# The whole issue order of a routed-attention and feed-forward kernel replaced: same operations, engines and buffers, another order of all five queues

## The chip, the cores and the metric

The kernel runs on one core of a Trainium2 chip. The core has five instruction queues that run beside each other: TensorE (PE in the profile, its weight loads as PEld), VectorE (DVE), ScalarE (ACT), GpSimd (POOL) and SyncE (SP), which here only issues transfers. Each queue runs its instructions strictly in the order in which they were written, and waits on semaphores for what other queues or transfers deliver. The metric is the device time of one execution in microseconds (us); lower is better.

## The reference, cut to what matters

Two stages follow each other. The first is attention for 4 batches, 8 heads, 768 tokens and a head size of 64, in which a query sees only the keys of its own cluster (the nearest of 16 centroids). Its output, 3072 tokens of 512 values, goes through a feed-forward stage with a softmax gate and a layer norm.

```python
mask = q_assign[:, :, :, None] == k_assign[:, :, None, :]
scores = scale * np.matmul(q, k.transpose(0, 1, 3, 2))
scores = np.where(mask, scores, -1000000000.0)
attn = softmax(scores)                    # over the keys
x = np.matmul(attn, v)                    # 3072 x 512 after a reshape
h = x @ w_in                              # 3072 x 1024
solu = h * softmax(h)
ln = (solu - mu) / np.sqrt(var + 1e-06) * g_ln
out = ln @ w_out                          # 3072 x 512
```

## The kernel before

The heads are worked off in pairs, four pairs in each of the four batches. Each step of the kernel is a small function with a name, added to a table with its engine and what it needs. The names that matter here, with batch `b`, pair `p`, `i` = 0 for queries and 1 for keys:

- `ld b.p.i` loads tokens (L381 for batch 0; L412 for the later batches, in four parts for two pairs at once, the last part without a number: `ld1.0.0` is the last part of the queries of batch 1, `ld1.0.1` that of the keys). `lv` loads values (L558), `lo0` to `lo3` load w_out (L599), `li0` and `li1` load the two halves of w_in with a cast and are issued by POOL (L583).
- `tp` and `xa`/`xt` turn tokens in batch 0 (on PE, L395), `xt` turns them in later batches (on DVE, L420). `cl` multiplies by the centroids (PE, L469); `tb`, `mx`, `oh`, `ot` make the cluster masks (DVE); `pl` puts these rows below the tokens (L541); `ca` casts the tokens (L438, L440); `cv` casts values (L566).
- `S` multiplies scores (PE, L644), `E` is the exponential of 1024 columns (ACT, L654, 144 of them), `V` multiplies by the values into the one bank `ob` (PE, L666), `N` divides by the sums and so frees `ob` (DVE, L678 and L689).
- `me`, `mk`, `mf`, `km`, `ce` centre w_out once: `mk` (DVE, L614) copies a sum out, `mf` (PE, L617) multiplies that copy.
- Of the feed-forward stage, for 24 blocks of 128 tokens: `tx` turns x by a transfer, `h` is the first product (PE, L777), `hm` the maximum (DVE, L787), `ex` the exponential (ACT, L803), `u` a product (POOL, L810), `tu` a turn by a transfer, `y` the second product (PE, L849), `as`, `bn`, `ag`, `al` the norm, `sc` the scaling and `ou` the store.
- `z1` to `z5` and `sg` are small constants set by POOL (L1327, L1311).

What sets the order is one hand-kept list, `ORDER` (L38), of all 1562 names. `Weave.run` goes through it and calls each function, so that the list gives each of the five queues its order at once:

```python
for name in ORDER:
    o = self.ops[name]
    assert done.issuperset(o["first"]) and name not in done, name
    ...
    o["fn"]()
    done.add(name)
```

A second table, `AWAY`, gives some steps to another engine than usual. The scores have two buffers of 1024 columns in PSUM, so PE can be two regions ahead of ACT; the products `h` have one bank each for their two halves; token tiles have four buffers. Transfers issued by SP are written into hardware queues in SP's order; POOL's transfers have a queue of their own (q0 in the profile, against q1 for SP's).

Of the kernel before, what the change touches and what calls it, by code (L numbers as in the profile page):

```python
# [43 lines left out]
tp0.2.0.1 xa0.2.0 ot0.0.1 cl0.1 z1 pl0.0.1.0 pl0.0.0.1 pl0.0.0.0 cv0.0.0 pl0.0.1.1.0 xt0.2.0 S0.0
pl0.0.1.0.1 S0.1 pl0.0.1.1.1 tb0.1 tp0.2.1.0 pl0.0.1.0.0 E0 S1.0 xa0.2.1 tp0.2.1.1 ca0.1.0.1 S1.1
xt0.2.1 cv0.0.1 tp0.3.0.0 ca0.2.0.0 S2.0 E1 mx0.1 S2.1 cl0.2 z4 oh0.1 ca0.2.1.0 E2 xa0.3.0 S3.0
S3.1 ot0.1 V0.0 tp0.3.0.1 E3 ca0.1.1.0 S4.0 S4.1 xt0.3.0 V0.1 ca0.2.1.1 V1.0 E4 V1.1 tb0.2 S5.0 lo0
S5.1 z2 pl0.1.1.1 N0 tp0.3.1.0 E5 S6.0 pl0.1.1.0 xa0.3.1 S6.1 V2.0 lo3 V2.1 mx0.2 pl0.1.0.1 E6
tp0.3.1.1 ld1.0.0.2 pl0.1.0.0 S7.0 ca0.1.1.1 gt xt0.3.1 S7.1 lv0.2 cv0.1.1 V3.0 V3.1 gk oh0.2 S8.0
E7 ca0.3.0.0 S8.1 cl0.3 N1 E8 ot0.2 cv0.1.0 S9.0 S9.1 gw V4.0 V4.1 E9 S10.0 pl0.2.0.1 pl0.2.0.0  # L50
S10.1 tb0.3 V5.0 ld1.0.0 V5.1 E10 sg S11.0 pl0.2.1.0 ld1.0.1.0 ca0.2.0.1 S11.1 N2 me0 E11 mx0.3
pl0.2.1.1 V6.0 V6.1 oh0.3 ca0.3.0.1 S12.0 S12.1 ca0.3.1.0 V7.0 S13.0 E12 ld1.0.1.1 S13.1 ot0.3
ca0.3.1.1 cv0.2.0 me1 E13 pl0.3.0.0 S14.0 pl0.3.1.0 cv0.2.1 lv0.3 S14.1 mk V7.1 E14 pl0.3.1.1 S15.0
N3 S15.1 mf z3 ld1.0.1.2 pl0.3.0.1 E15 ld1.0.1 S16.0 km S16.1 V8.0 V8.1 E16 li0 S17.0 ce2 S17.1
V9.0 V9.1 E17 S18.0 N4 S18.1 li1 ld1.2.0.0 E18 S19.0 S19.1 cv0.3.0 cv0.3.1 xt1.0.0 ld1.2.0.1 E19
V10.0 V10.1 ce1 V11.0 V11.1 S20.0 N5 S20.1 S21.0 E20 S21.1 V12.0 V12.1 xt1.0.1 E21 V13.0 S22.0
S22.1 ce3 ca1.0.1.0 V13.1 E22 S23.0 N6 S23.1 cl1.0 xt1.1.0 E23 ce0 S24.0 S24.1 ptx0 xt1.1.1 V14.0
V14.1 E24 V15.0 S25.0 S25.1 tx0 V15.1 E25 z5 ca1.1.0.0 S26.0 N7 S26.1 cl1.1 ce5 E26 tb1.1 S27.0
S27.1 tb1.0 V16.0 V16.1 E27 S28.0 mx1.0 S28.1 V17.0 V17.1 ld1.2.0.2 E28 ca1.0.0.0 S29.0 N8 S29.1
h0.0.0 oh1.0 E29 V18.0 ld1.2.0 S30.0 S30.1 h0.0.1 ot1.0 E30 S31.0 S31.1 ld1.2.1.0 V18.1 ce4 V19.0  # L60
E31 pl1.0.0.0 V19.1 S32.0 S32.1 N9 h0.1.0 ld1.2.1.1 E32 hm0.0 S33.0 pl1.0.1.1 S33.1 V20.0 h0.1.1
E33 ld1.2.1.2 pl1.0.1.0 S34.0 S34.1 V20.1 V21.0 E34 V21.1 pl1.0.0.1 S35.0 ld1.2.1 N10 S35.1 h1.0.0
E35 ca1.0.1.1 hm0.1 S36.0 S36.1 lv1.0 V22.0 xt1.2.0 h1.0.1 bl1.0 E36 S37.0 S37.1 hm1.0 ca1.0.0.1
V22.1 tx2 V23.0 E37 V23.1 S38.0 N11 S38.1 ca1.1.1.0 h1.1.0 E38 lv1.1 S39.0 ca1.2.0.0 S39.1 h1.1.1
tx4 E39 xt1.2.1 S40.0 ca1.1.1.1 S40.1 E40 hm1.1 cl1.2 xt1.3.0 cv1.0.0 ex0.0 S41.0 S41.1 cv1.0.1
V24.0 V24.1 tb1.2 V25.0 V25.1 E41 V26.0 u0.0 S42.0 V26.1 S42.1 N12 h2.0.0 E42 h2.0.1 xt1.3.1 V27.0
h2.1.0 ex1.0 ce6 tu0 S43.0 hm2.0 S43.1 h2.1.1 E43 V27.1 S44.0 hm2.1 ld2.0.0.0 S44.1 h3.0.0 E44
ld2.0.0.1 bn0.0 cl1.3 u1.0 bn0.1 lv1.2 ex2.0 V28.0 V28.1 tb1.3 S45.0 V29.0 V29.1 mx1.2 ld2.0.0.2
S45.1 h3.0.1 ca1.2.1.0 E45 ld2.0.0 S46.0 S46.1 oh1.2 h3.1.0 ca1.3.0.1 E46 y0.0 N13 h3.1.1 cv1.1.1
S47.0 S47.1 bn1.0 ca1.1.0.1 cv1.1.0 ld2.0.1.0 y0.1 E47 hm3.0 S48.0 S48.1 y0.2 ot1.2 E48 tu1 V30.0  # L70
S49.0 S49.1 ce7 V30.1 V31.0 E49 V31.1 ld2.0.1.1 S50.0 as0 as1 ca1.2.0.1 pl1.2.0.1 bn1.1 S50.1
h4.0.0 ld2.0.1.2 E50 hm3.1 S51.0 pl1.2.1.1 S51.1 V32.0 ag0 V32.1 E51 y0.3 pl1.2.1.0 N14 S52.0 S52.1
h4.0.1 ld2.0.1 pl1.2.0.0 al0 E52 S53.0 as2 S53.1 bl1.2 V33.0 u2.0 V33.1 E53 h4.1.0 lv1.3 hm4.0
# [1285 lines left out]
```

## Time and profile before

| | before |
|---|---|
| time, median of 3 runs | 220.64 us (220.5 to 221.01) |
| profiled execution, span from first to last instruction | 224.4 us |
| PE busy | 213.4 us (95%) |
| ACT busy | 190.0 us (85%) |
| DVE busy | 182.4 us (81%) |
| POOL busy | 162.3 us (72%) |
| moved by transfers | 37.28 MB, 120878 packets |

The profile gives the span alone for the profiled execution; it is 3.8 us longer than the median of the timed runs, although the span holds nothing ahead of the first or behind the last instruction. Busy time of PE is modelled at its ends: a matmul that waits inside the pipe counts as busy. Idle time of an engine is put down to what released it last.

### The profile page before, as it was taken

The page shows a single profiled execution, that of the slowest core. Times are in us where ns is not written, and L with a number is a line of the kernel's source. Part 1 is how long each engine was busy: PE and PEld are TensorE (multiplying, and loading weights), DVE is VectorE, ACT ScalarE, POOL GpSimd, SP SyncE. Part 2 cuts the span into 40 slices and gives each one's busy share as a digit, 9 for nine tenths or more (in the row PEclk, how much of TensorE's full clock was granted, in tenths as well). Part 3 has the DMA queues.
Part 4 walks back from the last instruction along what each step waited for, and adds up shares of the span by engine and source line. Part 5 has one row for each costly group of instructions (what it writes and reads, how often), then busy time and mean ns, then how long its engine had stood idle before and what let it go on. Part 6 is the DMA issues. An engine that isn't in the chain of part 4 may idle for free.

```text
span 224.4 us, 6272 instructions
## 1 busy us (share of the span) xinstructions
PE 213.4 (95%) x2400; PEld 149.4 (67%) x2431; DVE 182.4 (81%) x431; ACT 190.0 (85%) x239; POOL 162.3 (72%) x202
## 2 busy tenths in 40 slices
...
GB/s 212 386 350 225 171 179 201 170 174 104 50 75 179 149 184 212 181 214 177 216 147 275 164 157 102 169 116 173 113 209 96 94 34 165 133 167 128 189 61 142
DMA packets 120878, 37.28 MB, mean 166 GB/s; under 512 B 109960, under 2 KB 116368, under 8 KB 120848
## 3 DMA queue, kind: packets, MB, share of 16 engines
q1 hardware_dynamic: 119872, 35.31, 77.0%
q0 software_dynamic: 544, 1.05, 2.6%
...
## 4 chain that ended last, share of the span: by engine, by line
PE 81%; POOL 8%; DMA 4%; DVE 2%; issue 2%; SPq 0%; DVEq 0%; POOLq 0%
PE sb L644 24%; PE hb L777 17%; PE mb L849 16%; PE ob L666 13%; PE hb L469 5%; DMA raw<-in_k_dram 4%; POOL kbig L440 2%; POOL qbig L438 2%; PE hb L849 2%; PE sb L952 1%; POOL kbig L541 1%; POOL v L566 1%; POOL qbig L541 1%; PE hb L395 1%; DVE cst L483 0%
## 5 line engine op out<-in xcount | busy, mean ns | idle before, releaser
L654 ACT ACTIVATE e<-sb 128x1024 bf16<-128x1024 f32 x144 | 140.0, 1022 | 16.5 <-PE sb L644 15.2
L644 PE MATMUL sb<-qbig,kbig 80*128 80x256 bf16 (+3 forms) x648 | 85.3, 262 | 0.7 <-ACT e L654 0.3
L644 PEld LDWEIGHTS <-kbig 80*128 80x128 bf16 (+1 forms) x648 | 62.4, 120 | 25.3 <-issue 8.2
L810 POOL TENSOR_TENSOR u<-e_sb,w_st 128x1024 bf16<-128x1024 bf16 x21 | 45.1, 2147 | 18.7 <-ACT e_sb L803 12.3
L666 PEld LDWEIGHTS <-e 128*128 128x128 bf16 x1152 | 48.8, 98 | 12.3 <-issue 1.9
L666 PE MATMUL ob<-v,e 128*128 128x65 bf16 x1140 | 51.9, 193 | 0.4 <-DVE x L689 0.2
L777 PE MATMUL hb<-w_in_sb,xT 128*128 128x512 bf16 x172 | 50.4, 379 | 0.6
L849 PE MATMUL mb<-w_out_c,uT 128*128 128x512 bf16 x157 | 43.6, 379 | 0.6
L821 DVE BATCH_NORM_STATS2 bs<-u 128x6 f32<-128x512 bf16 x48 | 31.8, 681 | 1.1 <-POOL u L810 1.1
L803 ACT ACTIVATE e_sb<-w_st,nmax 128x1024 bf16<-128x1024 f32 (+1 forms) x25 | 27.9, 1114 | 5.5 <-DVE w_st L787 4.1
L440 POOL TENSOR_SCALAR kbig<-xt 64x768 bf16<-64x768 f32 (+1 forms) x30 | 27.4, 916 | 6.8 <-DVE xt L420 5.3
L438 POOL CAST qbig<-xt 64x768 bf16<-64x768 f32 (+1 forms) x32 | 26.7, 837 | 5.8 <-DVE xt L420 2.1
L420 DVE STREAM_TRANSPOSE xt<-raw 128x768 f32<-128x768 f32 x24 | 22.6, 961 | 5.3 <-DMA raw<-in_k_dram 5.2
L845 POOL TENSOR_TENSOR alpha<-var,halves 128x1 f32<-128x1 f32 x24 | 15.8, 659 | 11.8 <-DVE var L828 11.2
L849 PEld LDWEIGHTS <-uT 128*128 128x128 bf16 x176 | 15.2, 97 | 9.6
L777 PEld LDWEIGHTS <-xT 128*128 128x128 bf16 x192 | 16.1, 98 | 7.9
L787 DVE TENSOR_SCALAR_CACHE_REDUCE w_st<-hb,nmax 128x512 f32<-128x512 f32 x24 | 17.8, 743 | 3.2 <-PE hb L777 2.6
L689 DVE TENSOR_TENSOR x<-ob,den 128x256 bf16<-128x256 f32 (+2 forms) x40 | 19.0, 474 | 1.4
L787 DVE TENSOR_SCALAR_CACHE_REDUCE w_st<-hb 128x512 f32<-128x512 f32 x24 | 16.3, 679 | 4.1 <-PE hb L777 4.1
L678 DVE RECIPROCAL den<-ob 128x4 f32<-128x4 f32 (+2 forms) x40 | 7.2, 180 | 10.1 <-PE ob L666 9.6
L469 PE MATMUL hb<-xt,c_bd 128*32 128x384 f32 x96 | 11.4, 522 | 3.3 <-DVE xt L420 3.3
L541 POOL COPY qbig<-oht 32x768 f32<-32x768 f32 (+2 forms) x11 | 9.1, 824 | 6.5 <-DVE oht L508 3.3
...
## 6 DMA issues: line engine op xcount, KB each, us to landing
...
raw<-in_k_dram SPq DMA_DIRECT2D x26, 192.0 KB, 4.1
raw<-in_q_dram SPq DMA_DIRECT2D x24, 192.0 KB, 4.9
w_g<-in_moe_w_out_dram SPq DMA_DIRECT2D x4, 512.0 KB, 7.4
...
w_in_sb<-in_moe_w_in_dram POOLq DMA_DIRECT2D x2, 512.0 KB, 7.6
```

The lines of the kernel that those rows point to most:

```text
L438: (nc.vector if e == "DVE" else nc.gpsimd).tensor_copy(dst, src)
L440: (nc.vector if e == "DVE" else nc.gpsimd).tensor_scalar(dst, src, scalar1=inv_C, scalar2=1.0, op0=Alu.mult, op1=Alu.mult)
L469: nc.tensor.matmul(bank_of(t, n)[c * NB:(c + 1) * NB, :L], w, xts[b, p, i][:, c0 + x * L:c0 + (x + 1) * L] .rearrange("p (n q) -> p q n", ...
L644: nc.tensor.matmul(reg[:, c:c + wd], kb[u, pp, side_of(h), keys], qb[u, pp, side_of(h), su * P:su * P + wd])
L654: nc.scalar.activation(es[r][:, :w], src, Act.Exp, scale=exp_scale, bias=-exp_scale)
L666: nc.tensor.matmul(ops_of(group_of[n])[:, s, :VW], es[r][:, c0:c0 + P], v1[index[b, pair_of(h)] % R][:, side_of(h), kt, :VW], start=(kt == ...
L777: nc.tensor.matmul(hb[f2][:], xTs[f][:, dc, :], w_in_sb[:, dc, f2 * BANK:(f2 + 1) * BANK], start=(dc == 0), stop=(dc == n_dc - 1))
L787: nc.vector.tensor_scalar(ff[f, "h"][:, f2 * BANK:(f2 + 1) * BANK], hb[f2][:], scalar1=-1.0, scalar2=nmax[:, f2 - 1:f2] if f2 else 3.0e38, ...
L803: nc.scalar.activation(ff[f, "e"][:, cols(f, f2)], ff[f, "h"][:, cols(f, f2)], Act.Exp, bias=ff[f, "nmax"][:, n_ff2 - 1:], scale=-1.0, acc ...
L810: (nc.vector if e == "DVE" else nc.gpsimd).tensor_tensor(ff[f, "u"][:, cols(f, f2)], ff[f, "e"][:, cols(f, f2)], ff[f, "h"][:, cols(f, f2) ...
L821: nc.vector.bn_stats(ff[f, "bs"][:, f2, :], ff[f, "u"][:, f2 * BANK:(f2 + 1) * BANK])
L849: nc.tensor.matmul(y_of(f, x), ff[f, "uT"][:, fc, :], w_out_c[:, fc, parts_of(f, x)], start=(fc == 0), stop=(fc == n_fc - 1))
```

## The change

The list `ORDER` is replaced by another order of the same 1562 names; it was found by a search over replays of the kernel with varied durations. `AWAY` holds the same entries (only its line breaks differ), and all functions, buffers and engines stay. The file is one line shorter, so that line numbers behind the list are lower by one in the kernel after. Almost every row of the list moves; its first two lines show how:

```diff
 ORDER = """
-lc ld0.0.0.0 ld0.0.1.0 ld0.0.0 ld0.0.1 wu ld0.1.0 ld0.1.1 ld0.2.0 cx cy lv0.0 ld0.2.1 tp0.0.0.0 cz
-ld0.3.0 tp0.0.0.1 xa0.0.0 lg tp0.0.1.0 xt0.0.0 ca0.0.0.0.0 lv0.1 cp lo1 ca0.0.0.0.1 cb tp0.0.1.1
...
+wu z5 lc ld0.0.0.0 ld0.0.1.0 ld0.0.0 ld0.0.1 cx ld0.1.0 cy ld0.1.1 z3 tp0.0.0.0 cz lv0.0 z4 z2
+ld0.2.0 ld0.2.1 tp0.0.0.1 xa0.0.0 ld0.3.0 tp0.0.1.0 ca0.0.0.0.0 xt0.0.0 cp tp0.0.1.1 xa0.0.1 cb
...
```

Three places of it follow, each as the queue stood before and as it stands now. The first is POOL's queue near the end of the work on batch 0, where POOL issues the two halves of w_in (L583, L582 now). Before:

```order
L566 CAST v_2_104<-vf 128x6x64
L541 COPY kbig_100<-oht 32x384
L566 CAST v_2_104<-vf 128x6x64
L541 COPY kbig_100<-oht 32x384
L1327 MEMSET v_3_105 128x12x2
L541 COPY qbig_97<-oht 32x384
L583 DMA w_in_sb<-in_moe_w_in_dram 128x2x1024 x2
L566 CAST v_3_105<-vf 128x6x64
```

Now:

```order
L565 CAST v_2_104<-vf 128x6x64
L582 DMA w_in_sb<-in_moe_w_in_dram 128x2x1024
L565 CAST v_2_104<-vf 128x6x64
L540 COPY kbig_100<-oht 32x384
L437 CAST qbig_97<-xt 64x6x128
L540 COPY qbig_97<-oht 32x384
L439 TENSOR_SCALAR kbig_100<-xt 64x6x128
L540 COPY kbig_100<-oht 32x384
L565 CAST v_3_105<-vf 128x6x64
L582 DMA w_in_sb<-in_moe_w_in_dram 128x2x1024
```

The two halves, which stood together, are apart: one (`li1`) stands ahead of six casts and copies, the other (`li0`) behind them and behind the last value cast `cv0.3.1`.

The second is SP's queue up to the loads of batch 1; `raw_234` before and `raw_249` now hold batch 1's queries, `raw_508` and `raw_505` its keys, `w_g` is w_out, `vf` values. Before:

```order
L412 DMA raw_234<-in_q_dram 32x48x32 x2
L599 DMA w_g_110<-in_moe_w_out_dram 128x2x512 x2
L412 DMA raw_234<-in_q_dram 32x48x32
L558 DMA vf_424<-in_v_dram 128x2x384
L412 DMA raw_234<-in_q_dram 32x48x32
L412 DMA raw_508<-in_k_dram 32x48x32 x2
L558 DMA vf_574<-in_v_dram 128x2x384
L412 DMA raw_508<-in_k_dram 32x48x32 x2
```

Now:

```order
L411 DMA raw_249<-in_q_dram 32x48x32
L598 DMA w_g_110<-in_moe_w_out_dram 128x2x512
L557 DMA vf_301<-in_v_dram 128x2x384
L411 DMA raw_249<-in_q_dram 32x48x32
L598 DMA w_g_110<-in_moe_w_out_dram 128x2x512
L411 DMA raw_249<-in_q_dram 32x48x32
L598 DMA w_g_110<-in_moe_w_out_dram 128x2x512
L557 DMA vf_449<-in_v_dram 128x2x384
L411 DMA raw_249<-in_q_dram 32x48x32
L411 DMA raw_505<-in_k_dram 32x48x32 x4
```

The last value load of batch 0 (`lv0.3`) moved from between the key parts to ahead of the last query part; ahead of the last key part stands the same set of loads as before.

The third is DVE's queue at the same time. `y<-hb` are `mk` and `km`, `xt<-raw` turns batch 1's queries (`xt1.0.0`, needs `ld1.0.0`) and keys (`xt1.0.1`, needs `ld1.0.1`), `x<-ob,den` is `N`. Before:

```order
L440 TENSOR_SCALAR kbig_100<-xt 64x6x128
L514 STREAM_TRANSPOSE oht<-oh 128x3x64 x2
L541 COPY qbig_97<-oht 32x384
L614 COPY y<-hb_93 128x512
L678 RECIPROCAL den<-ob 128x4
L689 TENSOR_TENSOR x<-ob,den 128x2x2x64
L614 COPY y<-hb_92 128x512
L621 SCALAR_TENSOR_TENSOR w_out_c<-w_g,g_ln_111,y 128x512
L678 RECIPROCAL den<-ob 128x4
L689 TENSOR_TENSOR x<-ob,den 128x2x2x64
L566 CAST v_3_105<-vf 128x6x64
L420 STREAM_TRANSPOSE xt<-raw 128x768
```

Now:

```order
L513 STREAM_TRANSPOSE oht<-oh 128x3x64 x2
L419 STREAM_TRANSPOSE xt<-raw 128x768
L613 COPY y<-hb_93 128x512
L439 TENSOR_SCALAR kbig_100<-xt 64x6x128
L677 RECIPROCAL den<-ob 128x4
L688 TENSOR_TENSOR x<-ob,den 128x2x2x64
L540 COPY qbig_97<-oht 32x384
L565 CAST v_3_105<-vf 128x6x64
L613 COPY y<-hb_92 128x512
```

The turn of the queries moved from behind the last value cast to ahead of `mk`, so that `mk` and all that follows on DVE now stands behind a wait for `ld1.0.0`. The turn of the keys keeps its place: behind `N5` on DVE, and PE's `cl1.0`, which needs both turns, still stands between `S23` and `S24` with the same PE work ahead of it.

More of the change, by code (lines that the diff above doesn't have):

```diff
@@ L44 @@
[L44 to L73, printed above, removed]
```

175 lines of the change are left out of this document (102 added, 73 removed).

## The prediction

> **What bounds the kernel now.** I read the windows first, to see which stage has time to give. The columns are window, length, busy time of PE, PEld, DVE, ACT and POOL with the count of instructions, granted PE clock, share of the transfer engines and GB/s.
>
> ```profile
> PE 213.4 (95%) x2400; PEld 149.4 (67%) x2431; DVE 182.4 (81%) x431; ACT 190.0 (85%) x239; POOL 162.3 (72%) x202
> ...
> 60.00:220.00 160.00, 158.48 (x1784) 111.95 (x1813) 138.30 (x325) 143.41 (x184) 117.60 (x124) 1.00 0.79 151
> ...
> 40.40:43.80 3.40, 3.40 (x23) 1.91 (x24) 2.89 (x6) 0.90 (x1) 3.32 (x5) 0.50 0.96 153
> 41.00:46.00 5.00, 5.00 (x56) 3.17 (x52) 3.48 (x7) 2.17 (x3) 4.83 (x7) 0.72 1.12 180
> 26.00:30.00 4.00, 4.00 (x43) 2.24 (x42) 3.23 (x8) 3.72 (x5) 3.62 (x8) 1.00 0.68 105
> ```
>
> From 60 to 220 us PE is busy 158.48 of 160 at full clock: another order of the same matmuls can win next to nothing there and can only add waits. What can be won lies ahead of 60 us. There the waits and the order in time show one event:
>
> ```profile
> ACT e L654 <- PE sb L644: 15.2, 23, 5.4
> POOL kbig L440 <- DVE xt L420: 5.3, 1, 5.3
> DVE xt L420 <- DMA raw<-in_k_dram: 5.2, 1, 5.2
> PE hb L469 <- DVE xt L420: 3.3, 1, 3.3
> ```
>
> ```profile
> 27.84 9.70 ACT L654 ACTIVATE e<-sb 128x1024 bf16<-128x1024 f32 x10 [0.22 <-PE sb L644]
> ...
> 42.90 1.02 ACT L654 ACTIVATE e<-sb 128x1024 bf16<-128x1024 f32 x1 [5.37 <-PE sb L644]
> 44.85 3.92 ACT L654 ACTIVATE e<-sb 128x1024 bf16<-128x1024 f32 x4 [0.93 <-PE sb L644]
> ...
> 36.20 0.87 PE L469 MATMUL hb<-xt,c_bd 128*32 128x384 f32 x4
> 40.34 1.50 PE L469 MATMUL hb<-xt,c_bd 128*32 128x384 f32 x4 [3.27 <-DVE xt L420]
> ...
> 29.75 9.37 DMA raw<-in_k_dram
> ...
> 39.31 0.98 DVE L420 STREAM_TRANSPOSE xt<-raw 128x768 f32<-128x768 f32 x1 [5.25 <-DMA raw<-in_k_dram]
> ```
>
> The last key part, `ld1.0.1`, is issued at 29.75 and lands at 39.12. DVE stands at `xt1.0.1` for it, PE's `cl1.0` begins its key half at 40.34, and ACT and POOL run dry for over 5 us. Behind the wait PE runs at clock 0.50 for 3.4 us, which costs 1.7 more. Ten exponentials took 9.70, so back to back E24 and E25 would have begun at 37.54 and 38.51; E25 began at 44.85. The event costs 6.3 us, and all engines stand still together, so what is won here should reach the end.
>
> **Why that load is late.**
>
> ```profile
> q1 hardware_dynamic: 119872, 35.31, 77.0%
> q0 software_dynamic: 544, 1.05, 2.6%
> ...
> w_in_sb<-in_moe_w_in_dram POOLq DMA_DIRECT2D x2, 512.0 KB, 7.6
> ...
> 29.24 1.15 SPq L412 DMA_DIRECT2D raw<-in_k_dram  x2
> raw<-in_k_dram SPq DMA_DIRECT2D x1, 192.0 KB, 4.2
> ...
> 20.14 2.77 SPq L412 DMA_DIRECT2D raw<-in_q_dram  x1
> raw<-in_q_dram SPq DMA_DIRECT2D x1, 192.0 KB, 7.5
> ```
>
> The part issued just before, at 29.24, landed after 4.2 us, at 33.4. 192 KB at the 180 GB/s of the window from 41 are 1.1 us, so the last part was due at 34.5; it came 4.6 later. In between ran w_in, q0: 2.6% of 224.4 are 5.8 us of all 16 engines, 2.9 for each half. A q0 packet takes 2.6% x 16 x 224.4 / 544 = 172 ns, a q1 packet 77% x 16 x 224.4 / 119872 = 23 ns. The Trainium skill (DMA: Bandwidth & Descriptors, Queues, rings and completion order) states that each engine takes turns between queues packet by packet; turn by turn q1 would get 23 of 195 ns, an eighth. By that rule the loads all but stop while w_in moves, wherever it is put, and only w_in moved behind the load would help; the 4.6 us here agree.
>
> **The change, part by part.** First, w_in on POOL.
>
> ```profile
> 25.03 1.03 POOL L438 CAST qbig<-xt 64x768 bf16<-64x768 f32 x1
> ...
> 27.23 0.54 POOL L566 CAST v<-vf 128x384 bf16<-128x384 f32 x1
> ...
> 30.45 1.70 POOL L583 DMA_DIRECT2D w_in_sb<-in_moe_w_in_dram  x2 [0.24 <-issue]
> 32.40 0.61 POOL L566 CAST v<-vf 128x384 bf16<-128x384 f32 x1 [0.25 <-DMA vf<-in_v_dram]
> L1327 POOL MEMSET v<- 128x24 bf16 x5 | 0.6, 119 | 0.1
> ```
>
> The six instructions that `li1` now stands ahead of lie between 25.03 and 30.45, less the 0.54 of `cv0.2.0` and a memset of 0.12: 4.8 us. It is issued at about 25.7. `li0` stands behind the same work plus `cv0.3.1` (0.61), less the memsets now done at the start (0.6 together, while POOL waits): about 31, where the second half stood before.
>
> By bytes the loads ahead of `ld1.0.1` are the same set, so it is due at 34.5 plus 2.9 for the first half, less what that half finds idle: in 26 to 30 the engines were busy 0.68, idle 1.3 us. That is 36.1. The second half, landing 7.6 after issue of which 5.8 are movement of both, starts some 2 us after 31, at 33, ahead of 36.1. So the landing lies between 36.1 (the second half does not get in its way) and 39.0 (all 2.9 added). I take 38.0, nearer to the second row, since in the profile w_in did hold back a load that was already issued. Then DVE and PE follow in 1.2 as before: `cl1.0` at 39.2.
>
> Second, the turn of the queries ahead of `mk` on DVE.
>
> ```profile
> 25.30 1.17 DVE L440 TENSOR_SCALAR kbig<-xt 64x768 bf16<-64x768 f32 x1
> 26.39 0.62 DVE L514 STREAM_TRANSPOSE oht<-oh 128x192 f32<-128x192 f32 x2
> 27.43 0.69 DVE L614 COPY y<-hb 128x512 f32<-128x512 f32 x1
> ...
> 28.20 1.10 PE L617 MATMUL hb<-y,fold 128*128 128x512 f32 x2
> ...
> GB/s 212 386 350 225 171 179 201 170 174 104 50 75 179 149 184 212 181 214 177 216 147 275 164 157 102 169 116 173 113 209 96 94 34 165 133 167 128 189 61 142
> ```
>
> DVE reaches it at 27.0 less the 1.17 that stand behind it now: 25.8. Its load landed at 27.6 and now has `lv0.3` ahead too, 384 KB, which at 180 GB/s would be 2.1, and 1.0 at the 386 of the page's second slice, in which such loads run alone. I take 1.4: 29.0. The turn ends 1.2 later, `mk` at 30.9 instead of 28.12. PE stands at `mf` meanwhile: E16, which began 1.7 after `mk` ended, begins at 32.6, and nine exponentials at 0.97 later E25 at 41.3. PE's gap before `cl1.0` shrinks to about half a microsecond, since PE arrives some 2.8 later than at 36.6. So this wait lies inside the first one and costs nothing by itself; if the keys land early it sets the end, and the gain is at most 44.85 - 41.3 = 3.5.
>
> With PE's gap so short I count no slow clock; 4.5 us from `cl1.0` to E25 become 2.8, and E25 begins at 42.0: a gain of 2.8, between 0 (landing at 39.1, slow clock and all) and 6.3 (no wait at all). The Trainium skill (TensorE: Matmul & The Clock Gate, Part 1) puts the half clock down to a whole idle window of about 3.4 us; here an idle 3.3 to 3.8 us had it, so by that rule 1.7 us go with a gap below it, whenever the keys land.
>
> Third, the order from 60 us on. An example is the division `N14` on DVE, which frees `ob`:
>
> ```profile
> 74.47 0.20 DVE L678 RECIPROCAL den<-ob 128x6 f32<-128x6 f32 x1
> ...
> 76.97 0.69 DVE L787 TENSOR_SCALAR_CACHE_REDUCE w_st<-hb 128x512 f32<-128x512 f32 x1
> ...
> 78.02 0.97 DVE L420 STREAM_TRANSPOSE xt<-raw 128x768 f32<-128x768 f32 x1
> ```
>
> Now a turn (0.97), a maximum (0.69) and two small ones come ahead of it, over 1.7 us later against `V33`, with about half a microsecond more matmul in between. Such places cost between 0 (another engine is ahead anyway) and 1.5; I take 0.5 for all of them. The end is the same: `y23`, a scaling, a store:
>
> ```profile
> 219.64 1.04 PE L849 MATMUL ob<-w_out_c,w_g 128*128 128x256 bf16 x8
> ...
> 220.79 0.48 DVE L864 TENSOR_SCALAR w_g<-ob,alpha 128x256 f32<-128x256 f32 x1 [0.92 <-PE ob L849]
> ```
>
> The two halves of `y23` are interleaved now, which leaves the last scaling where it is: 0, between -0.2 and 0.5.
>
> **The sum.** Profiled: 224.4 - 2.8 + 0.5 = 222.1. The median is 3.8 under the span. If these 3.8 lie elsewhere, the change gives 220.64 - 2.3 = 218.3. If they all lie in this wait, which alone hangs on transfers, 2.5 of its 6.3 are left, and of these the same share, 1.1, is won: 220.0. I take 219.4, nearer to the second, because PE work cannot differ by as much.
>
> **The rivals.** (a) No change. The keys land behind both halves of w_in, at 39.0, as the skill's turn-by-turn rule has it; the same bytes come first in either order. Then E25 keeps its time but for the clock, which the 0.5 of the third part eats: 220.6. For it speaks that `li0` starts at 31 in either kernel, against it that `li1` uses time in which the engines were idle. (b) Slower. `li1`, issued at 25.7 and moving 2 us later, gets ahead of the last query part, which DVE now needs early. The load lands 2.9 later, at 31.9; `mk`, `mf` and all later exponentials follow, E25 at 31.9 + 12.3 = 44.2. Against the profile's 44.85 that is -0.6, against a timed run whose wait is 3.8 shorter (E25 at 41.05) +3.1; with the 0.5 of the third part -0.1 to +3.6, and I say the middle, +1.7: 222.3. On the second reading it decides from a landing of `ld1.0.0` at 41.05 - 12.3 = 28.8. For it speaks the 7.5 us of that load, against it that SP issues it earlier. (c) The wait goes whole and the third part costs nothing: 217.5.
>
> **Chances.** My forecast 0.46, (c) 0.07, (a) 0.21, (b) with its like in the third part 0.26. A measurement of this kernel tells about 0.2% (0.44 us) from no change. Forecast and (c) are faster: 0.53; (a) is the same: 0.21; (b) slower: 0.26. The range runs from 217.2 (under (c)) to 222.4 (over (b)'s price); the forecast's own range is 218.3 to 220.1.
>
> **What would show it.** Right: `xt<-raw` of the keys starts at 36 to 38.5, PEclk stays at 1.00 from 36 to 46, ACT's longest wait is under 3 us, and w_in's two issues stand over 4 us apart. DVE waits for `raw<-in_q_dram` at 26 to 29. Wrong: the keys land at 39 or later; or `mk` ends after 31.5 and ACT stands dry near 30; or PE's busy share between 60 and 215 falls under 98%, with DVE's `den` or `xt` as releaser.

## The result and the profile after

The kernel after takes 229.69 us (median of 4 runs, 227.71 to 230.26), the kernel before 220.58 beside it (4 runs, 220.5 to 221.01). The ratio is 1.0375, with a 95% interval of 1.0302 to 1.0447: 8.3 us slower by the ratio (6.7 to 9.9), 9.1 by the medians. The ratio leaves out executions over 1.5% above the fastest of the same kernel, the medians count them all. My forecast was 219.4, in a range of 217.2 to 222.4.

One thing has to be known first. The execution of before that the prediction read (span 224.4) was not like the timed ones. The time of a run is its span plus about 1.8 us (227.71 against a span of 225.9, 230.26 against 228.5), so that execution took some 226 us, by my estimate, and not 220.6. Such a long one is rare: of the 58 executions of before that were timed beside the other kernels 57 took 220.14 to 221.5 us, and one 229.09. Below, after is read against an ordinary execution of before (first experiment, span 218.5, 220.33 us). The page of that one, and then the page of after, busy time and first waits:

```profile
span 218.5 us, 6303 instructions
PE 212.5 (97%) x2431; PEld 147.7 (68%) x2431; DVE 182.4 (83%) x431; ACT 190.0 (87%) x239; POOL 161.6 (74%) x202
```

```profile
span 228.5 us, 6310 instructions
PE 216.4 (95%) x2431; PEld 148.8 (65%) x2431; DVE 184.9 (81%) x431; ACT 190.6 (83%) x239; POOL 158.6 (69%) x202
```

The span is 10.0 longer: PE is idle for 12.1 us instead of 6.0, and is called busy 3.9 us longer for the same 2431 matmuls. The Trainium skill (Perfetto Trace Analysis, Summary: the profiler window per engine type) says that a TensorE window runs from the start of its reading to an end that is only estimated. The 3.9 agree with that if a part of the waiting is counted as work, and e7 below shows one product for which it is. PE's idle time is therefore taken as a lower bound of its waits.

Where the idle time lies is seen in stretches of the span (windows). The columns are window, length, busy time of PE, PEld, DVE, ACT and POOL, granted PE clock, share of the transfer engines and GB/s. First before (ordinary execution), then after:

```profile
0.00:40.00 40.00, 37.73 (x439) 24.90 (x439) 32.76 (x81) 32.19 (x41) 33.52 (x66) 1.00 1.01 247
40.00:60.00 20.00, 20.00 (x262) 14.66 (x258) 15.88 (x35) 19.85 (x23) 15.43 (x18) 1.00 0.80 138
60.00:80.00 20.00, 20.00 (x245) 15.25 (x238) 19.41 (x42) 19.45 (x25) 19.14 (x21) 1.00 1.04 181
...
160.00:200.00 40.00, 40.00 (x479) 27.32 (x477) 31.43 (x83) 33.24 (x42) 21.00 (x23) 1.00 0.63 123
```

```profile
0.00:40.00 40.00, 35.48 (x383) 23.36 (x383) 27.62 (x72) 29.16 (x37) 27.50 (x60) 1.00 1.03 244
40.00:60.00 20.00, 19.02 (x259) 14.02 (x258) 16.62 (x31) 17.29 (x20) 14.42 (x18) 1.00 0.93 163
60.00:80.00 20.00, 18.61 (x203) 12.77 (x196) 18.73 (x39) 18.01 (x25) 18.54 (x19) 1.00 0.82 148
80.00:100.00 20.00, 19.95 (x259) 15.09 (x258) 18.91 (x40) 18.90 (x23) 15.26 (x16) 1.00 1.08 205
100.00:120.00 20.00, 19.56 (x231) 13.91 (x230) 15.39 (x36) 18.96 (x24) 16.86 (x22) 1.00 0.90 128
120.00:140.00 20.00, 19.24 (x240) 14.24 (x237) 18.92 (x38) 18.80 (x22) 17.82 (x20) 1.00 1.03 201
140.00:160.00 20.00, 19.78 (x219) 13.47 (x217) 16.73 (x40) 18.85 (x25) 14.50 (x17) 1.00 0.47 108
160.00:200.00 40.00, 40.00 (x495) 28.67 (x494) 29.90 (x79) 35.69 (x45) 22.03 (x24) 1.00 0.50 113
```

The loss is in no single place. Before has 20.00 in each window of 20 us from 40 to 160. In after PE has 2.25 us less ahead of 40, and 0.05 to 1.4 less in each window from 40 to 160; from 160 to 200 it is as full as before. The clock is 1.00 in all of them.

The opening can be followed on DVE. Its timeline in after (start, time, what, and the idle time ahead of it with what ended it):

```profile
30.10 0.98 DVE L419 STREAM_TRANSPOSE xt<-raw 128x768 f32<-128x768 f32 x1 [2.54 <-DMA raw<-in_q_dram]
31.00 0.65 DVE L613 COPY y<-hb 128x512 f32<-128x512 f32 x1
...
40.32 1.84 DVE L419 STREAM_TRANSPOSE xt<-raw 128x768 f32<-128x768 f32 x2 [2.51 <-DMA raw<-in_k_dram]
```

and in the ordinary execution of before:

```profile
27.22 0.69 DVE L614 COPY y<-hb 128x512 f32<-128x512 f32 x1
...
32.47 0.97 DVE L420 STREAM_TRANSPOSE xt<-raw 128x768 f32<-128x768 f32 x1
...
33.89 0.97 DVE L420 STREAM_TRANSPOSE xt<-raw 128x768 f32<-128x768 f32 x1
```

Before turned the queries at 32.47 and the keys at 33.89 and waited for neither. After waits 2.5 us for each. ACT shows what it costs, after first and before second (the rows begin with E16 and with E24):

```profile
33.37 7.67 ACT L653 ACTIVATE e<-sb 128x1024 bf16<-128x1024 f32 x8 [1.72 <-PE sb L643]
43.17 2.85 ACT L653 ACTIVATE e<-sb 128x1024 bf16<-128x1024 f32 x3 [2.13 <-PE sb L643]
```

```profile
29.63 7.70 ACT L654 ACTIVATE e<-sb 128x1024 bf16<-128x1024 f32 x8 [0.15 <-PE sb L644]
37.52 1.02 ACT L654 ACTIVATE e<-sb 128x1024 bf16<-128x1024 f32 x1 [0.19 <-PE sb L644]
```

E0 is 1.4 us late already (13.36 against 11.94), E16 3.7 and E24 5.65. The other 4.4 of the 10.0 us come behind E24, in waits such as these on PE (`h4`, `y4` and V57):

```profile
72.25 0.61 PE L776 MATMUL hb<-w_in_sb,xT 128*128 128x512 bf16 x2 [0.73 <-DMA xT<-x]
...
100.87 1.02 PE L848 MATMUL mb<-w_out_c,uT 128*128 128x512 bf16 x4 [0.42 <-ACT y L861]
...
123.93 0.36 PE L665 MATMUL ob<-v,e 128*128 128x65 bf16 x6 [0.76 <-DVE x L688]
```

The waits on PE of 0.2 us and more behind E24 are six, with `h2`, V68 and one at the end, and add up to 3.0 of these 4.4 us; the ordinary execution of before has none there.

### The profile page after: what moved, and what is told of

Read it like the earlier page. It is cut to its first block, busy times and chain, and to the rows that moved or that the text cites. A ratio compares the mean times of both kernels' runs of the same rounds, so it can differ in the third digit from the quotient of the medians.

```text
span 228.5 us, 6310 instructions
## 1 busy us (share of the span) xinstructions
PE 216.4 (95%) x2431; PEld 148.8 (65%) x2431; DVE 184.9 (81%) x431; ACT 190.6 (83%) x239; POOL 158.6 (69%) x202
## 4 chain that ended last, share of the span: by engine, by line
PE 53%; POOL 15%; DMA 12%; DVE 11%; SPq 4%; issue 2%; ACT 0%; DVEq 0%; POOLq 0%
PE sb L643 15%; PE hb L776 12%; PE mb L848 11%; PE ob L665 8%; DMA raw<-in_k_dram 4%; POOL u L809 4%; DMA vf<-in_v_dram 3%; DMA raw<-in_q_dram 3%; SPq L411 2%; POOL w_out_c L626 2%; PE hb L468 2%; POOL kbig L439 2%; POOL qbig L437 2%; DVE bs L820 2%; DVE oh L498 2%
## 5 line engine op out<-in xcount | busy, mean ns | idle before, releaser
L643 PE MATMUL sb<-qbig,kbig 80*128 80x256 bf16 (+3 forms) x648 | 92.9, 262 | 0.5 <-ACT e L653 0.3
L643 PEld LDWEIGHTS <-kbig 80*128 80x128 bf16 (+1 forms) x648 | 61.4, 120 | 25.1 <-issue 7.4
L665 PEld LDWEIGHTS <-e 128*128 128x128 bf16 x1152 | 52.8, 97 | 15.8 <-issue 2.6
L665 PE MATMUL ob<-v,e 128*128 128x65 bf16 x1140 | 57.6, 193 | 1.1 <-DVE x L688 1.0
L776 PE MATMUL hb<-w_in_sb,xT 128*128 128x512 bf16 x192 | 54.7, 379 | 1.4 <-DMA xT<-x 0.7
L848 PE MATMUL mb<-w_out_c,uT 128*128 128x512 bf16 x168 | 47.4, 379 | 0.4 <-ACT y L861 0.4
L844 POOL TENSOR_TENSOR alpha<-var,halves 128x1 f32<-128x1 f32 x24 | 13.4, 561 | 21.7 <-DVE var L827 16.8
L439 POOL TENSOR_SCALAR kbig<-xt 64x768 bf16<-64x768 f32 (+1 forms) x30 | 24.8, 828 | 2.6 <-DVE xt L419 0.6
L540 POOL COPY kbig<-oht 32x768 f32<-32x768 f32 (+2 forms) x17 | 11.9, 701 | 5.9 <-DVE oht L507 4.9
L861 ACT ACTIVATE y<-mb,alpha 128x512 f32<-128x512 f32 x12 | 8.2, 688 | 5.4 <-PE mb L848 4.4
```

The lines of the kernel that those rows point to most:

```text
L439: (nc.vector if e == "DVE" else nc.gpsimd).tensor_scalar(dst, src, scalar1=inv_C, scalar2=1.0, op0=Alu.mult, op1=Alu.mult)
L643: nc.tensor.matmul(reg[:, c:c + wd], kb[u, pp, side_of(h), keys], qb[u, pp, side_of(h), su * P:su * P + wd])
L665: nc.tensor.matmul(ops_of(group_of[n])[:, s, :VW], es[r][:, c0:c0 + P], v1[index[b, pair_of(h)] % R][:, side_of(h), kt, :VW], start=(kt == ...
L776: nc.tensor.matmul(hb[f2][:], xTs[f][:, dc, :], w_in_sb[:, dc, f2 * BANK:(f2 + 1) * BANK], start=(dc == 0), stop=(dc == n_dc - 1))
L848: nc.tensor.matmul(y_of(f, x), ff[f, "uT"][:, fc, :], w_out_c[:, fc, parts_of(f, x)], start=(fc == 0), stop=(fc == n_fc - 1))
```

## The experiments

"Over before" is the ratio less one, times 220.6, with its 95% interval. An order cut at a step means: all names up to it as in the one list, and then the names that are left in the sequence of the other. Such a kernel has a seam that neither list has, and what the seam costs is in its number.

| kernel | median, us | over before, us |
|---|---|---|
| after | 229.69 | 8.3 (6.7 to 9.9) |
| e2 new opening (to E26) | 226.92 | 5.2 (3.6 to 6.8) |
| e18 new middle (E26 to E108) | 228.04 | 8.2 (6.5 to 9.9) |
| e4 new end (from E108) | 222.76 | 2.3 (1.6 to 3.0) |
| e3 new middle and end | 228.03 | 6.8 (5.8 to 7.8) |
| e5 SP's new queue alone | 233.28 | 12.3 (11.3 to 13.3) |
| e6 queries' turn alone | 221.64 | 1.2 (0.8 to 1.6) |
| e7 w_in halves alone | 221.61 | 0.7 (0.2 to 1.2) |
| e8 first centroid product alone | 220.84 | 0.4 (0.1 to 0.8) |
| e10 these three together | 222.68 | 2.3 (1.1 to 3.4) |
| e11 and SP's new opening | 224.06 | 2.9 (1.9 to 4.0) |
| e12 turns of x late, alone | 222.24 | 1.4 (0.8 to 2.0) |
| e13 after, opening's three undone | 228.37 | 7.4 (6.5 to 8.3) |
| e14 after, divisions undone | 228.79 | 8.4 (7.7 to 9.1) |
| e15 after, turns of x undone | 227.66 | 7.0 (5.4 to 8.5) |
| e16 after, all of these undone | 225.77 | 5.4 (4.4 to 6.4) |
| e17 and the old end | 226.70 | 5.7 (4.8 to 6.6) |

### Is the wait for the keys in every execution of before?

The kernel before, unchanged, profiled once more.

> The kernel before, unchanged, for a second profile. Theory 1 (the profile that I predicted from was a disturbed execution: the wait for the keys of batch 1 is not in an ordinary run): a time of 220.6 and a span near 219, ACT's longest wait between exponentials under 1.5 us, exponential E24 (the 25th) beginning at 37.5 to 38.5 instead of 42.9, PE clock 1.00 throughout. Theory 2 (the wait is in every run, and the span is simply counted otherwise): a span near 224 again with ACT idle for over 5 us near 38 to 43.

220.33 us, span 218.5: theory 1, with E24 at 37.52. DVE took the keys at 33.89 without a wait (row above), and PE went through `cl1.0` in one piece:

```profile
36.00 0.88 PE L469 MATMUL hb<-xt,c_bd 128*32 128x384 f32 x8
```

The wait of 5.3 us is not in this execution, which is at the median. SP's and POOL's timelines show what differs. Ordinary execution:

```profile
28.30 1.43 SPq L412 DMA_DIRECT2D raw<-in_k_dram  x2
30.44 1.70 POOL L583 DMA_DIRECT2D w_in_sb<-in_moe_w_in_dram  x2 [0.44 <-issue]
```

Here the issue of the keys' last part ends at 29.73, 0.7 us ahead of the first half of w_in, and the keys are in by 33.89. In the execution of the prediction it ended at 29.24 + 1.15 = 30.39, 0.06 us ahead of 30.45, and the keys landed at 39.12. What the transfer engines did there from 33.5 to 37 us, while the keys were outstanding (queue, packets, MB, share of 16 engines):

```profile
q0 software_dynamic: 331, 0.65, 103.5%
q1 hardware_dynamic: 170, 0.02, 7.1%
```

w_in, on q0, had the engines, and all of SP's loads, on q1, moved 0.02 MB in 3.5 us. The Trainium skill (DMA: Bandwidth & Descriptors, Queues, rings and completion order) has each engine take turns between queues packet by packet, by which, as I had estimated, q1 is left with about an eighth of the time in the middle of w_in. The 7.1% are of that size; the packets, 170 to 331, are not one for one, and whether a packet of the profile is a packet of that rule no run here shows.

Which execution gets the long wait looks like a race between two queues, but the distance of the issues does not decide it alone. In e17, whose profiled execution (231.07) was that run's longest, the issue of the keys ended at 31.35, 0.58 us behind the start of w_in's at 30.77. In e5 it ended at 30.45, 0.05 behind 30.40, and in e13 at 31.59, 0.23 behind 31.36. DVE's turns of the keys in these three:

```profile
40.73 0.98 DVE L419 STREAM_TRANSPOSE xt<-raw 128x768 f32<-128x768 f32 x1 [5.43 <-DMA raw<-in_k_dram]
34.57 0.97 DVE L419 STREAM_TRANSPOSE xt<-raw 128x768 f32<-128x768 f32 x1
35.95 1.84 DVE L419 STREAM_TRANSPOSE xt<-raw 128x768 f32<-128x768 f32 x2 [0.30 <-DMA raw<-in_k_dram]
```

So between 0.58 us behind w_in's start and 0.06 ahead of it both outcomes are on record, and where the keys' issue ended 0.68 us or more ahead (e1, e3, e4, e6, e8, e12, e16, e18) none of the profiles has the wait. What decides in between is not known.

### Which stretch carries the loss?

```diff
-ORDER of before
+e2: the order of after up to E26, then that of before
+e3: the order of before up to E26, then that of after
+e4: the order of before up to E108, then that of after
```

> The new order up to exponential E26, the old order from there. Theory 1 (an ordinary run of before has no wait in the opening, and the new opening brings three: product cl0.0 behind a load, mk behind the queries' load, the keys behind both halves of w_in): 5 to 6 us over before, about 226. Theory 2 (what is lost is lost behind 60 us, where the matmuls had no idle time before): within 1 us of before, 220 to 221.5.

> The old order up to E26, the new order from there: the complement of the run before. Theory 1: 3 to 4 us over before, about 224, the two parts adding up to the 9.1 of the whole change. Theory 2: about 229, the whole loss.

> The old order up to E108 (about 146 us), the new order from there. If the loss of the later part lies in the end (the profile after shows h23 3.5 us later against the exponentials than before): nearly all of what e3 loses, 2.5 to 3.5 us. If it lies in the middle (E48 to E80 came 2.8 us later): under 1 us.

Over before: 5.2, 6.8 and 2.3 us. The opening is as theory 1 had it, the rest lies between the theories (3 to 4 and about 9), and the end has about a third of the rest. Each stretch, put into the old order, is slower, also those behind 60 us where I had seen PE full. Opening and rest make 12.0, the whole order 8.3: they do not add. Part of it may be the seams. Another part is that a late opening gives the loads behind it more time, so that waits of the rest go into it. One place shows it, `h2` on PE, in e3 (profiled in its longest execution, 230.19) and then in after:

```profile
59.52 1.04 PE L776 MATMUL hb<-w_in_sb,xT 128*128 128x512 bf16 x4 [1.77 <-DMA xT<-x]
```

```profile
62.34 1.02 PE L776 MATMUL hb<-w_in_sb,xT 128*128 128x512 bf16 x4 [0.66 <-DVE cst L482]
```

In after PE comes 2.8 us later, and the transfer is no longer what it waits for.

### SP's queue by itself

```diff
-SP: the queue of before
+SP: the queue of after, all of it; PE, DVE, ACT and POOL as before
```

> The kernel before with one queue exchanged whole: SP, which issues the loads, the turns of x and the stores, gets its new order; PE, DVE, ACT and POOL keep the old one. Theory 1 (the new order puts loads and turns close to their use, and on the chip they land later than it reckons): tx2 and tx4 stand behind the loads of batch 2, and the last value load of batch 0 ahead of the queries of batch 1, as in the order after; the old compute queues, which ask a little earlier, wait at h2 and h4 for 1 to 2 us each: 3 to 7 us slower, 224 to 228. Rival 2 (the loss is made by the orders of the compute queues, which stand in each other's way, and transfers only follow): within 0.7 us of before, 220.0 to 221.4, and no wait on xT over 0.5 us.

12.3 us over before, slower than after itself and far above either theory's numbers. PE's largest single wait ends at 142.83, and the clock is 0.83 in the window in which it ends:

```profile
140.00:160.00 20.00, 17.17 (x161) 10.76 (x162) 12.22 (x26) 13.90 (x19) 10.11 (x12) 0.83 0.60 122
```

```profile
142.83 1.03 PE L848 MATMUL mb<-w_out_c,uT 128*128 128x512 bf16 x2 [5.57 <-DMA uT<-u]
```

and SP's timeline shows why:

```profile
122.09 12.17 SPq L557 DMA_DIRECT2D vf<-in_v_dram  x3
...
134.82 4.05 SPq L411 DMA_DIRECT2D raw<-in_k_dram  x3
138.97 1.83 SPq L815 DMA_TRANSPOSE uT<-u  x1
```

SP stands 12 us at three value loads (`lv3.0` to `lv3.2`): the third is issued only at 133.9, when a cast of values on POOL that began at 133.4 is done. Behind them come the parts of a key load, and only then `tu7`, which PE's old queue needs by 137. This shows that the new order of SP does not fit the old compute queues. It does not show how much of the loss of after is SP's, so the run does not decide between the theories.

### The three moves of the prediction, one at a time

```diff
 e6, DVE: pl0.3.0.0
+xt1.0.0
 mk ... cv0.3.0
-xt1.0.0
 N5
```

> The kernel before with one step moved on one queue: on DVE the turn of the queries of batch 1 (xt1.0.0) stands ahead of mk, as in the order after; its load keeps its place on SP. Theory 1: in the ordinary execution of before that load lands at 28.0 while mk begins at 27.2, so the turn takes 28.0 to 29.0, mk 29.1 to 29.8, mf begins at 30.4 instead of 28.5, PE stands for it, and as PE has no slack behind it, 1.3 to 2.2 us reach the end: 222.0 to 222.9. Rival 2 (as my forecast had it: a wait here costs nothing by itself, since later waits take it up): within 0.5 us of before, 220.2 to 221.2.

1.2 us over before (0.8 to 1.6): theory 1, a little under its 1.3 to 2.2. DVE does not wait for the load here: the turn begins at 27.71, as soon as DVE is free, and its own time puts `mk` at 28.61 instead of 27.22. PE waits for `mk` in `mf`:

```profile
29.32 1.12 PE L616 MATMUL hb<-y,fold 128*128 128x512 f32 x2 [0.57 <-DVE y L613]
```

and the loss is in the time, against my "costs nothing by itself".

```diff
 e7, POOL: cv0.2.0
+li1
 pl0.3.1.0 ... pl0.3.0.1
+cv0.3.1
 li0
-li1
-cv0.3.1
```

> The kernel before with POOL's two halves of w_in placed as in the order after: li1 behind the value cast cv0.2.0, li0 behind cv0.3.1; every other queue is as before. Theory 1: the half that moves 4 to 5 us earlier holds back the loads issued with it, the keys of batch 1 land some 2 to 3 us later than the 33.9 of before, at 36 to 37, PE arrives at their product at 36.0 and waits 1 to 2 us: 221.3 to 222.7. Rival 2 (PE's queue ahead of it has enough to do, or the halves use idle engines, as my forecast had it): within 0.5 us of before, 220.2 to 221.2.

0.7 us over before (0.2 to 1.2), between the theories in size; the median, 221.61, is in theory 1's range, and two of the ten executions took 224.25 and 226.61. The profiled one, 221.64, has theory 1's mechanism, on DVE and then on PE:

```profile
36.17 0.98 DVE L419 STREAM_TRANSPOSE xt<-raw 128x768 f32<-128x768 f32 x1 [2.35 <-DMA raw<-in_k_dram]
36.19 1.88 PE L468 MATMUL hb<-xt,c_bd 128*32 128x384 f32 x8
```

The keys are taken at 36.17 instead of 33.89, and `cl1.0`, which took 0.88 us in the ordinary execution of before (row above), is busy for 1.88 at the same clock of 1.00: PE's wait for the keys is counted as work. The split that I had counted as a gain makes the keys 2.3 us later than an ordinary execution of before has them.

```diff
 e8, PE: tp0.0.1.1
+tp0.1.0.0
 cl0.0
-tp0.1.0.0
 tp0.1.0.1
```

> The kernel before with one step moved on PE: the turn tp0.1.0.0 of the tokens of the second pair stands ahead of the first centroid product cl0.0, as in the order after. Theory 1 (the start of the new order costs by PE's queue): cl0.0 waits for a load it doesn't need, begins 0.6 to 1.3 us later, E0 as much, and all of it reaches the end: 221.2 to 222.0. Rival 2 (the start is late because of SP's order, values ahead of tokens): E0 moves by less than 0.4 us, 220.2 to 221.0.

0.4 us over before (0.1 to 0.8): less than theory 1's 0.6 to 1.3, and a time that rival 2 has too (220.0 to 221.0). The profiled execution, the longest of ten (221.86), has theory 1's wait, `cl0.0` (`mb`) now behind a turn that waits for a load, and E0 at 13.67 instead of 11.94; how late E0 is in an ordinary one is not on record:

```profile
8.20 0.52 PE L393 MATMUL hb<-ident_f,raw 128*128 128x128 f32 x3 [1.02 <-DMA raw<-in_q_dram]
8.65 0.55 PE L467 MATMUL mb<-xt,g_wide 128*32 128x192 f32 x8
```

### Do they add up?

```diff
 e10: the edits of e6, e7 and e8 together
 e11: these, and SP's queue as after up to lv1.0, then as before
```

> The kernel before with the three moves tried alone put together: xt1.0.0 ahead of mk on DVE, the halves of w_in where the order after has them on POOL, tp0.1.0.0 ahead of cl0.0 on PE. SP, and everything else, is as before. They cost 1.2, 0.7 to 1.1 and 0.4 alone. Theory 1 (each makes PE wait at a place of its own, and PE has no slack to give it back): they add up, 222.6 to 223.4. Rival 2 (an earlier wait covers a later one, since the loads have more time then): 221.4 to 222.3, not above the turn alone by more than 0.6.

> The same three moves, and SP's new order from its start to the first value load of batch 1 (lv0.0 ahead of the tokens of the third pair, lv0.2 and lv0.3 ahead of the queries of batch 1); behind that SP is as before. SP's new order cost under 1 us in the opening where the other queues were old. Theory 1 (it is the combination that costs: the turn now stands early on DVE, and its load stands one 384 KB load later on SP): the load lands at 29 to 30 instead of 28.0, the keys at 36 or later, E24 begins 4 to 6 us late, 224 to 227, near the 226.9 of the whole new opening. Rival 2 (SP's opening is harmless here too, and the new opening loses by the remaining moves of its casts and copies): within 0.7 us of the three moves without it.

2.3 us (1.1 to 3.4) where the three alone make 1.2 + 0.7 + 0.4 = 2.3: as if they added, though the interval is too wide to exclude rival 2. With SP's new opening it is 2.9 (1.9 to 4.0), not to be told from e10. The median of its four times, 224.06, just reaches theory 1's 224 to 227; by the ratio it is 223.5. The trace, of its shortest execution (222.92), has the late load, a wait of 0.59 us ahead of the queries' turn at 29.01, but E24 begins at 40.17, 2.65 us late and not the 4 to 6 that theory 1 had for it.

So rival 2 is the better one, without being settled. The whole new opening (5.2) costs 2.3 more than e11 by the middle values, with intervals that touch; which of its casts and copies make these was not tried.

### The turns of x late

```diff
 e12, SP: lv1.0
-tx2
 lv1.1
-tx4 tu0
 ld2.0.0.0 ld2.0.0.1
-lv1.2
 ld2.0.0.2 ld2.0.0
+tx2 tu0
 ld2.0.1.0
+lv1.2 tx4
 tu1
```

> The kernel before with two steps moved on SP alone: the turns of x by transfer tx2 and tx4 stand behind the loads of batch 2's first queries (ld2.0.0), tx4 also behind tu0, ld2.0.1.0 and lv1.2, as in the order after. Theory 1 (SP puts them into the hardware queue behind 768 KB and more of loads, they land behind those): tx2 is issued at 54 to 57 instead of 47.7, PE stands 2 to 3 us for h2, whose old place is at 56.0, and 0 to 1 for h4: 222.3 to 224.5. Rival 2 (other matmuls and the two score buffers cover it): within 0.6 us of before.

`tu0` and the value load `lv1.2` move with the two turns. 1.4 us over before (0.8 to 2.0), a little under theory 1's range; three of the ten executions took 224.84 to 226.34. The profiled one is of these (224.84), so that the size of its wait is not that of an ordinary one. SP issues `tx2` late, and PE waits for it at `h2`:

```profile
55.31 1.47 SPq L715 DMA_TRANSPOSE xT<-x  x1
...
58.77 1.04 PE L775 MATMUL hb<-w_in_sb,xT 128*128 128x512 bf16 x3 [2.41 <-DMA xT<-x]
```

In the ordinary execution of before SP issued it at 47.73.

### After once more

> The kernel after, unchanged, profiled once more: its first profile is of its longest execution (230.26), and its four executions lie 2.5 us apart, those of before half a us. Theory 1 (the loss lies at the same places in each execution, and the spread comes from when loads land): this one takes 227 to 230, E24 begins 3.5 to 6 us later than the 37.5 of before, and the waits ahead of h2, h4, y4 and V57 are there again, 0.5 to 1 us each. Rival 2 (the first profile caught waits that are not the rule): one or more of these places show no wait, and E24 is within 2 us of before.

227.71 us, span 225.9. Neither theory whole. The keys were taken at 35.87 instead of 40.32. The first profile of after has SP's issue of the keys' four parts and w_in's second half so:

```profile
24.33 9.49 SPq L411 DMA_DIRECT2D raw<-in_k_dram  x4
33.34 0.78 POOL L582 DMA_DIRECT2D w_in_sb<-in_moe_w_in_dram  x1
```

There the last part's issue ends at 33.82, with the second half of w_in already begun; in the second profile it ends at 29.38, against 33.06. What held SP so long in the first is not known. E24 began 2.0 late instead of 5.65, at rival 2's edge:

```profile
39.54 2.85 ACT L653 ACTIVATE e<-sb 128x1024 bf16<-128x1024 f32 x3 [0.35 <-ACT e L653]
```

Ahead of `h4` there is no wait either; the others of theory 1 (`h2`, `y4`, V57) are there again. Yet the end is 7.4 late instead of 10.0, so 5.4 are lost behind E24, and again six waits on PE of 0.2 us and more make 3.6 of them. The longest is at V44, for the division that frees `ob`:

```profile
95.76 0.62 PE L665 MATMUL ob<-v,e 128*128 128x65 bf16 x15 [1.28 <-DVE x L688]
```

The first profile of after does not have this one. What the keys do not cost in the opening is partly lost again in the middle.

### The new middle alone

```diff
-ORDER of before
+e18: before up to E26, after up to E108, then before
```

> The new order from E26 to E108 alone, old ahead of it and behind it. Theory 1 (the parts of the rest add: 7.3 for all behind E26 less 2.2 for the end): 5.1 us over before, 224.7 to 226.7. Rival 2 (the middle's waits are made up later, where the old end has room): under 3 us over before, 221.5 to 223.5.

8.2 us over before (6.5 to 9.9), above theory 1's 4.1 to 6.1, and as much as the whole new order. Its end in the new order costs nothing on top (e3: 6.8), though the new end alone costs 2.3. The first of its waits is one that after does not have, for a copy on POOL, so that a part of the 8.2 may be the seam's:

```profile
51.49 0.60 PE L642 MATMUL sb<-qbig,kbig 80*128 80x256 bf16 x4 [1.55 <-POOL qbig L539]
```

### The moves taken back inside the new order

```diff
 e13: DVE xt1.0.0 behind cv0.3.0; POOL li0 li1 ahead of cv0.3.1; PE cl0.0 ahead of tp0.1.0.0
 e14: DVE N18 behind ot2.0, N23 behind ot2.2, N27 behind ag7
 e15: SP tx2 tx4 behind lv1.1
 e16: all of these, and y23.1.0 to y23.1.3 ahead of y23.0.0
 e17: e16 up to E108, then the order of before
```

> The kernel after with the three moves of the opening taken back: xt1.0.0 behind cv0.3.0 on DVE, li0 and li1 together ahead of cv0.3.1 on POOL, cl0.0 ahead of tp0.1.0.0 on PE. Theory 1 (they cost in the new order what they cost in the old one): 2 to 3.5 us are won, 226.2 to 227.7. Rival 2 (the waits behind them, at h2, h4 and V44, grow by what is won, since their loads don't come earlier): less than 1 us is won, 228.7 to 229.9.

> The kernel after with three divisions on DVE moved up: N18 to behind ot2.0 (one copy earlier), N23 to behind ot2.2 (a statistics step and a copy earlier), N27 to behind ag7 (a copy and a turn earlier). Ahead of V44, V57 and V68, which wait for them, PE stood 0.9 to 1.4, 0.9 and 0.4 us in the traces of after. Theory 1 (DVE's order there is the cause): 1.5 to 2.7 us are won, 227.0 to 228.2. Rival 2 (what is moved behind the divisions is late for the scores instead): less than 0.7 us is won, 229.0 to 230.0.

> The kernel after with tx2 and tx4 back ahead of the loads of ld2.0.0 on SP; SP then waits at tx2 for its x before it issues them. Theory 1: the waits ahead of h2 and h4 go, 0.9 us each in the first trace, 0.9 and none in the second: 0.9 to 1.8 us are won, 227.9 to 228.8. Rival 2 (h2 waited there for DVE's turn of the centroid products in the same bank, not for the transfer): less than 0.5 us is won, 229.2 to 229.9.

> The kernel after with all of these taken back: the opening's three moves, the three divisions, tx2 and tx4, and the two halves of y23 one behind the other as in before. Everything else is in the new order. Theory 1 (these few moves carry most of the loss): 2 to 3.5 from the opening, 1.5 to 2.7 from the divisions, 0.9 to 1.8 from the turns, 0.4 from y23: 221.3 to 224.9. Rival 2 (the loss is spread over many places of an order in which every step comes just when its predecessor is due): 225.5 to 228.

> The kernel with all the moves taken back as in the run before it, and besides all steps behind E108 in the old order. Theory 1 (the new end costs its own 2.2 whatever stands ahead of it, less the 0.4 of y23 that is taken back already): 1.5 to 2.2 us under 225.8, 223.6 to 224.3. Rival 2 (the end's order only follows what the middle leaves, so that the seam costs as much as it wins): 225.0 to 226.5.

After is 8.3 over before. With the opening undone it is 7.4 (rival 2's size), with the turns of x undone 7.0 (theory 1's): both inside after's interval, so neither gain is settled. What the opening's moves win is seen again at `h2`, PE's timeline of e13:

```profile
59.50 1.04 PE L776 MATMUL hb<-w_in_sb,xT 128*128 128x512 bf16 x3 [1.76 <-DMA xT<-x]
```

In the first profile of after the idle time at `h2` was 0.66, in e3 1.77: in these three, the earlier PE comes there, the longer it waits. It need not be so: in the second profile of after PE comes at 58.04, nearly as early as in e3 and e13 (57.7), and waits 0.72. With the divisions moved up nothing is won (8.4), as rival 2 had it: the waits at V57 and V68 are gone and PE waits 0.16 us at V44 (1.28 in the second profile of after, none in the first), but 0.95 close by, ahead of `S72`, where neither profile of after waits. The profile names a step on POOL as what ended that; the copy `pl2.0.0.0` on DVE, which S72 needs and which stands behind the division in either order, ended 0.15 us before. PE's row and DVE's:

```profile
100.53 0.61 PE L643 MATMUL sb<-qbig,kbig 80*128 80x256 bf16 x4 [0.95 <-POOL alpha L844]
99.83 0.55 DVE L540 COPY qbig<-oht 32x768 f32<-32x768 f32 x1
```

With one copy more behind the division the copies are late for S72: rival 2's course, as far as this one place shows it. All together win 2.9 us (5.4 over before, 4.4 to 6.4), rival 2 of that run, and the old end behind them wins nothing (5.7), rival 2 again, though the median lies just above its numbers. No version came out under before.

## Why the prediction was wrong

The forecast missed by 10.3 us. The gain that I had from the wait makes some 1.7 of them (219.4 is 220.6 less 1.7 plus 0.5); the other 8.6 lie in terms that I had at nothing or at 0.5.

**The step that failed first: the offset between profile and median, and with it what there was to win.** I saw that the span was 3.8 above the median, gave 3.8 us to "elsewhere" or to a part of the wait, and kept at least 2.5 us of the wait in the ordinary run. The row that contradicted this was in the prediction: PE idle for 3.3 us and at half clock behind it. I also set a span against a time: with the 1.8 us that lie outside the span, the execution was 5.6 over the median, not 3.8, which is nearly the 6.3 of the event. Taken out of 224.4, these leave 218.1, and the ordinary span was 218.5. So none of the wait was in the median, as the profile of e1 has it. The term "0 to 6.3, taken as 2.8" was 0, and my forecast's and rival (c)'s gains fell with it; the 217.5 of (c) has no working in the prediction. What I had of the clock held: it is 1.00 from 36 to 46 us in after, where PE's wait for the keys is 0.93, and 0.64 from 41 to 45 in the profile of e17, where it is 3.84.

**w_in and the keys.** The mechanism was right, the reference was not. w_in does hold back the keys (7.1% of the engines' time were left to q1). With the split their turn is at 40.32 and 35.87 in the two profiles of after, so that neither lies in my 36 to 38.5; the first is on the side that I had set as "wrong". I had the halves issued at 25.7 and 31, they are at 27.66 and 33.34, and I had not reckoned with an issue of the keys that ends only at 33.82. But before's ordinary execution has its keys ahead of both halves. The same split is a loss of 0.7 us there.

**The turn of the queries ahead of `mk`.** I took the load at 29.0 and E16 at 32.6; in the first profile of after `ld1.0.0`'s turn began at 30.10 and E16 at 33.37. PE waits 1.29 us for `mk` there. The price "nothing by itself" hung on the later wait for the keys. I wrote what happens if that cover is gone, "it sets the end", but did not put the price into the sum for ordinary runs. Alone, in the order before, the move costs 1.2 us. The list's first 25 us, in which E0 already comes 1.4 us late, had no term in the prediction at all.

**The order from 60 us on.** Priced at 0.5 (0 to 1.5). In after PE has 2.9 us less from 60 to 160 by the windows (1.39 + 0.05 + 0.44 + 0.76 + 0.22), before what is hidden in its busy time; behind E24 its two profiles lose 4.4 and 5.4, and the new middle alone costs 8.2. The premise, PE full from 60 to 220, was right and I said that only losses are possible there; but I worked out one place (`N14`), where neither profile of after waits, and gave all others its price. The waits are at `h2`, `h4`, V44, V57 and `y4`, released by SP's transfers, by DVE and by ACT in turn, each 0.4 to 1.3 us. This was the largest mis-sized term.

**The end.** I had 0 (-0.2 to 0.5) for the last places; the whole new end from E108 costs 2.3 alone, and none on top of the new middle. The two interleaved halves of `y23` by themselves were not tried.

**The rivals.** (b), slower, had the right sign and two of its places, the queries' load and "its like in the third part", with 0.26. Its 222.3 and the range's 222.4 were far too low, since it added one mechanism where every stretch had its own. Of my signs, ACT's longest wait is 2.1 (I had set under 3 as "right"), which shows how little that one tells; w_in's issues, 5.7 us apart, and the clock stood on the "right" side too. `mk` ending at 31.65 stood on the "wrong" one. PE's share from 60 to 215 is 98.2% in the first profile of after and 97.2% in the second, on either side of the 98 that I had set, where the ordinary execution of before has 99.9%: two points are 3 us.

**What stays open.** The moves that were named carry 2.9 of 8.3 us. The other 5.4 are in the order of the opening's casts and copies and of the middle between 40 and 160 us. Single waits can be named there, and on PE behind E24 they make about two thirds of the loss (3.0 of 4.4 and 3.6 of 5.4), but which rows of the list make them was not found, and taking them away moves them, as with the divisions. That the search's replays had other durations than the chip is an explanation that no run here tested.
